# Latent attention with column-tiled score and value matmuls and one eviction for four heads

## Chip, cores and metric

The kernel runs on one core of a Trainium2 chip. The metric is the device time of one execution in microseconds, lower is better. The engines are TensorE (PE, with its weight loads as PEld), VectorE (DVE), ScalarE (ACT), GpSimd (POOL) and SyncE (SP), which issues the DMA transfers.

## The reference

Attention through 32 packed latents per head feeds two feed-forward blocks. All of it is float32.

```python
# q, k, v: 8 x 8 x 576 x 64   p: 8 x 8 x 32 x 64   (batch, heads, sequence, head_dim)
def sm_attn(qq, kk, vv):
    s = scale * np.matmul(qq, kk.transpose(0, 1, 3, 2))
    s = s - np.max(s, axis=-1, keepdims=True)
    a = np.exp(s)
    a = a / (np.sum(a, axis=-1, keepdims=True) + 1e-09)
    return np.matmul(a, vv)
p_packed = sm_attn(p, k, v)                  # the latents: the stage that is changed
out = sm_attn(q, p_packed, p_packed)
...
x = attn_out.transpose(0, 2, 1, 3).reshape(B * S, H * D)       # 4608 x 512
x = _moe_ref(x)     # rms norm, silu(x w_gate) * (x w_val), w_out; hidden 1536
return _moe2_ref(x) # h = x w_in; (h * cos(h)) w_out; hidden 2048
```

## The kernel before, in words

The program has three parts. The first computes the latents p_packed for all batches, four heads at a time: 16 groups (NG), one round of a loop (L535) for each, and two more rounds to finish. The second projects the latents through the gate and value weights, attends with the queries and runs the first feed-forward block. The third runs the second feed-forward block. Everything in the first part runs under a manual schedule, so each engine takes its instructions in the order in which the code issues them.

A round i of the first part works on several groups at once, in this order on TensorE: `u_et(i-1)` transposes the exponentials of the group before (tile et, evicted to eT), `u_s1(i)` multiplies latents with keys (the scores, tile s1, shown as s in the trace), `u_prep(i+1)` transposes the latents of the next group (tile pt), `u_kt(i+1)` transposes its keys in two halves (tile kp, evicted to kT by ScalarE), `u_fin(i-2)` transposes a finished result (tile tp), and `u_pp(i-1)` multiplies exponentials with values (tile pp, evicted to cd by VectorE). Pieces of the query attention of batch 0 (tiles qtp, sp, atp, xp, rp) are put between them.

The latents enter the scores as a block-diagonal operand pbd, so that one matmul over 128 rows serves two heads (64 rows each). There are two such pairs, j = 0 and 1. Before the change, pbd is 384 columns wide and mostly zeros: pair j is multiplied as 128 weight columns, of which 64 hold the two heads, and the second pair is added onto the first in the same PSUM tile. For the values, one matmul takes all four heads' exponentials (128 weight columns) against all four heads' values (256 columns); of the 128 x 256 result only the four diagonal blocks of 32 x 64 are wanted, and four VectorE operations take them out. The exponentials come in six chunks of 96 sequence positions.

Between the maxima and the transposes stands a chain over engines: s to VectorE (maximum, L403 and L404), to ScalarE (exponential e, L411), back to TensorE (et, L423). VectorE and ScalarE also convert weights in this stage (`w_prep`, tiles wy and ny), and GpSimd copies each k tile into another layout (`u_copy`, kc from kn) before TensorE transposes it. Keys and values are loaded a few rounds ahead (`load_k(i+3)`, `load_v(i+2)`, three buffers each), by DMAs that all stand in one SyncE queue, behind weight loads that wait for a buffer.

Of the kernel before, what the change touches and what calls it, by code (L numbers as in the profile page):

```python
# [9 lines left out]
F32 = mybir.dt.float32  # L10
# [3 lines left out]
ALU = mybir.AluOpType  # L14
# [6 lines left out]
def kernel(  # L21
# [14 lines left out]
    nc = tc.nc  # L36
    B, H, S, D = q.shape
    NP = p.shape[2]
# [4 lines left out]
    NC_ = S // CP  # L43
    HALF = S // 2
# [15 lines left out]
    BG_B, KP_B, ET_B, PP_B = 1, 2, 2, 1  # L60
# [114 lines left out]
    u1 = ust.enter_context(tc.tile_pool(name="u1", bufs=1))  # L175
# [5 lines left out]
    ps_1 = pst.enter_context(tc.tile_pool(name="ps_1", bufs=1, space=PSUM))  # L181

    gT = u1.tile([128, H], F32, name="gT")
    ppT = [mid_p.tile([128, 2, H, 128], F32R, name=f"ppT{i}") for i in range(B // 4)]
    pbd = [u1.tile([128, 384], F32, name=f"pbd{i}") for i in range(2)]
    for t in pbd:
        nc.gpsimd.memset(t, 0.0)

# [176 lines left out]
    def u_prep(i):  # L365
        pn, kc = nat_k.pop(i)[0], nat_c.pop(i)
        z = st[i] = {}
        pt = ps_2.tile([128, 128], F32, tag="kp", name="pt")
        nc.tensor.transpose(pt, pn.rearrange("p a d -> p (a d)"), ident)
        for r in range(2):  # L370
            rows = slice(r * 64, (r + 1) * 64)
            src, dst = (
                t[rows].rearrange("p (j x) -> p j x", j=2)[:, :, r * NP:(r + 1) * NP] for t in (pt, pbd[i % 2])
            )
            nc.vector.tensor_copy(dst, src)
        z["kT"], z["kc"] = u4.tile([128, 2, S], F32, tag="kT", name="kT"), kc
# [14 lines left out]
    def u_s1(i):  # L391
        z = st[i]
        kT = z["kT"]
        pb = pbd[i % 2]
        s1 = ps_1.tile([128, 2, 512], F32, tag="s1", name="s1")
        for hf in range(2):
            for j in range(2):
                nc.tensor.matmul(
                    s1[:, hf, :HALF], pb[:, j * 128:(j + 1) * 128], kT[:, j, hf * HALF:(hf + 1) * HALF],
                    start=j == 0, stop=j == 1,  # L400
                )
        mx = u2.tile([128, 4], F32, tag="mx", name="mx")
        nc.vector.tensor_reduce(out=mx[:, 0:1], in_=s1[:, :, :HALF], op=ALU.max, axis=AX.XY)  # L403
        nc.vector.tensor_scalar(out=mx[:, 1:2], in0=mx[:, 0:1], scalar1=-scale, scalar2=None, op0=ALU.mult)  # L404
        z["s1"], z["mx"] = s1, mx
# [23 lines left out]
    def u_pp(i):  # L429
        b, g = divmod(i, 2)  # L430
        z = st[i]
        eT, vn, mx = z["eT"], nat_v.pop(i), z["mx"]
        pp = ps_1.tile([128, 4, D], F32, tag="pp", name="pp", bufs=PP_B)
        for c in range(NC_):
            nc.tensor.matmul(pp, eT[:, c], vn[:, :, c, :], start=c == 0, stop=c == NC_ - 1)  # L435
        cd = u2.tile([128, 2, D], F32, tag="cd", name="cd")
        for h in range(4):
            r = slice(h * NP, (h + 1) * NP)
            src = pp[r, h, :].unsqueeze(1).to_broadcast([NP, 2, D])
            nc.vector.tensor_scalar(out=cd[r], in0=src, scalar1=mx[r, 3:4], scalar2=None, op0=ALU.mult)  # L440
        nc.sync.dma_start(out=c_dram[b][:, g, :], in_=cd[:, 0, :])
        z["cd"] = cd

# [85 lines left out]
    order.enter_context(tc.manual_schedule())  # L529
    u_copy(0)  # L530
    u_prep(0)
    u_kt(0, range(2))
    u_copy(1)
    w_q = [[], []]
    for i in range(NG + 2):  # L535
# [9 lines left out]
        if i < NG:  # L545
            u_s1(i)
        if i + 1 < NG:
            u_prep(i + 1)
            u_kt(i + 1, [0])
# [11 lines left out]
        if 0 < i <= NG:  # L561
            u_pp(i - 1)
# [126 lines left out]
    def gv_block(b, hf, f):  # L689
        w = wm_t[b, f // 2]  # L690
        a = ap_t[b, hf]
        fo = (f % 2) * 128
        pss = []
        for gv in range(2):
            ps = ps_gv.tile([128, HALF], F32, tag="mm", name=f"gv{gv}")
            for kt in range(2):
                mm3(
                    ps, w[gv][:, 0, kt, fo:fo + 128], w[gv][:, 1, kt, fo:fo + 128],
                    a[:, 0, kt], a[:, 1, kt], kt == 0, kt == 1,
                )  # L700
            pss.append(ps)
        t = f2.tile([128, HALF], F32, tag="silu", name="silu")
        nc.scalar.activation(out=t, in_=pss[0], func=AF.Sigmoid)
        nc.vector.tensor_tensor(out=t, in0=t, in1=pss[0], op=ALU.mult)  # L704
        nc.vector.tensor_tensor(out=t, in0=t, in1=pss[1], op=ALU.mult)  # L705
        return t
# [129 lines left out]
    for i in range(len(seq) + LAG):  # L836
        b, hf, f = seq[min(i, len(seq) - 1)]
        j = i % B1
        if i < len(seq):
# [12 lines left out]
            t = gv_block(b, hf, f)  # L852
# [8 lines left out]
        if i >= LAG:  # L861
            acc_block(*seq[i - LAG])
            att_step(2 * i + 1)
            b, hf, f = seq[i - LAG]
# [15 lines left out]
            b, hf, f = seq[min(i, len(seq) - 1)]  # L880
# [97 lines left out]
    for i in range(len(seq) + LAG_B):  # L978
        if i < len(seq):
            n, f = seq[i]  # L980
# [9 lines left out]
        if LAG_B <= i < len(seq) + LAG_B - T_END:  # L990
            n, f = seq[i - LAG_B]
# [33 lines left out]
```

## Time and profile before

| what | value |
|---|---|
| time, median of 3 runs | 1802.52 us |
| lowest and highest run | 1800.96 and 1807.84 us |
| profiled execution, first to last instruction (span) | 1799.0 us |
| span below the median of the runs | 3.5 us |
| TensorE busy over the span | 1709.1 us (95%) |
| VectorE, ScalarE, GpSimd busy | 1142.5, 895.8, 317.7 us |
| last eviction cd of the first part | ends at 167.6 us |

Busy times are sums over instructions of one profiled execution. Matmuls are pipelined, so a busy TensorE may still wait for its own results. An fp32 matmul appears as two records, each with a weight load; records of one matmul overlap the next, so the duration of a record is longer than the place that it takes in a row of matmuls. The granted clock of TensorE is a share of its full 2.4 GHz.

### The profile page before, as it was taken

The numbers are of one execution on the slowest core, as the hardware profiler recorded it, in microseconds if no ns is written. First come the engines' busy times: TensorE is split into PE (matmuls) and PEld (weight loads), VectorE is DVE, ScalarE is ACT, GpSimd is POOL, SyncE is SP. The second block draws the span as 40 slices with busy tenths as digits, with TensorE's granted clock in tenths as the row PEclk, the third lists the DMA queues.
The fourth block names the chain that finished last, engine by engine and source line by source line (L and its number), as shares of the span: only waits on it lengthen the run. The fifth ranks groups of instructions, "written<-read, shape, count | busy, mean of one in ns | idle before, by whom it ended". The sixth has DMA issues, their size and how long they took to land.

```text
span 1799.0 us, 26870 instructions
## 1 busy us (share of the span) xinstructions
PE 1709.1 (95%) x10144; PEld 1532.1 (85%) x10144; DVE 1142.5 (64%) x2188; ACT 895.8 (50%) x1725; POOL 317.7 (18%) x250
## 2 busy tenths in 40 slices
PE   7887787879999999999999999999999999999998
PEld 5665687879999999999999988888888888888887
DVE  3676488747676767676656756565656556555554
ACT  3445665534444444444444645454545555454444
POOL 3333666540303030303031300000000000000000
PEclk9988888989999999999999999999999999999999
DMA  9973677744343434343213401010101010100000
GB/s 221 240 191 112 192 243 219 216 148 140 92 139 90 136 94 138 94 140 91 101 55 118 138 1 48 0 48 0 47 1 48 1 47 14 34 1 24 1 24 24
DMA packets 119980, 166.92 MB, mean 93 GB/s; under 512 B 26921, under 2 KB 84265, under 8 KB 119849
## 3 DMA queue, kind: packets, MB, share of 16 engines
q1 hardware_dynamic: 119848, 165.19, 31.0%
q8 instruction: 80, 1.31, 0.3%
q14 instruction: 52, 0.42, 0.1%
HBM read 108.79 MB, written 53.22 MB: 90 GB/s over the span
## 4 chain that ended last, share of the span: by engine, by line
PE 79%; DVE 7%; DMA 7%; ACT 3%; issue 2%; SPq 1%; POOL 1%; ACTq 0%; DVEq 0%; POOLq 0%
PE ops L156 7%; PE ops L154 7%; PE hp L156 7%; PE hp L154 7%; PE hp L155 7%; PE ops L155 7%; PE acc L154 4%; PE acc L155 4%; PE acc L156 4%; PE gv L154 4%; PE gv L156 4%; PE gv L155 4%; DMA m<-ev 2%; PE pp L435 2%; DMA raw<-in_moe_w_in_dram 2%
## 5 line engine op out<-in xcount | busy, mean ns | idle before, releaser
L154 PE MATMUL gv<-apt,wmhl 128*128 128x288 f32 x768 | 233.6, 304 | 11.2 <-DVE silu L704 8.6
L154 PE MATMUL acc<-shl,wohl 128*128 128x288 f32 x768 | 237.1, 309 | 4.7 <-ACT wohl L106 4.5
L155 PE MATMUL acc<-shl,wohl 128*128 128x288 f32 x768 | 231.5, 301 | 0.1
L156 PE MATMUL acc<-shl,wohl 128*128 128x288 f32 x768 | 230.9, 301 | 0.5 <-POOL wohl L107 0.5
L156 PE MATMUL gv<-apt,wmhl 128*128 128x288 f32 x768 | 226.8, 295 | 1.8 <-POOL wmhl L107 1.8
L155 PE MATMUL gv<-apt,wmhl 128*128 128x288 f32 x768 | 227.1, 296 | 0.0
L154 PE MATMUL ops<-w2hl,ghl 128*128 128x512 f32 x576 | 224.2, 389 | 0.0
L155 PE MATMUL hp<-xhl,wmhl 128*128 128x512 f32 x576 | 224.1, 389 | 0.0
L156 PE MATMUL hp<-xhl,wmhl 128*128 128x512 f32 x576 | 224.1, 389 | 0.0
L155 PE MATMUL ops<-w2hl,ghl 128*128 128x512 f32 x576 | 224.1, 389 | 0.0
L154 PE MATMUL hp<-xhl,wmhl 128*128 128x512 f32 x576 | 224.1, 389 | 0.0
L156 PE MATMUL ops<-w2hl,ghl 128*128 128x512 f32 x576 | 222.7, 389 | 0.0
L107 POOL TENSOR_TENSOR wmhl<-wmraw,wmhl 128x512 fp32r<-128x512 f32 x100 | 128.4, 1305 | 512.9 <-ACT wmhl L106 505.6
L945 DVE TENSOR_TENSOR r<-r,hp 128x512 f32<-128x512 f32 x144 | 98.9, 687 | 186.6 <-ACT r L944 186.6
L943 ACT ACTIVATE r<-r 128x512 f32<-128x512 f32 x144 | 91.0, 632 | 247.6 <-DVE r L942 247.6
L106 ACT ACTIVATE shl<-silu 128x288 fp32r<-128x288 f32 x192 | 85.3, 444 | 241.1 <-DVE silu L705 239.9
L938 ACT ACTIVATE kk<-hp,magic 128x512 f32<-128x512 f32 x144 | 99.3, 689 | 122.5 <-PE hp L156 122.5
L154 PEld LDWEIGHTS gv<-apt,wmhl 128*128 128x128 f32 x768 | 144.9, 189 | 13.8 <-DVE silu L704 10.5
L154 PEld LDWEIGHTS acc<-shl,wohl 128*128 128x128 f32 x768 | 148.2, 193 | 5.0 <-ACT wohl L106 4.6
L155 PEld LDWEIGHTS acc<-shl,wohl 128*128 128x128 f32 x768 | 148.6, 194 | 0.6 <-DVE shl L107 0.5
L156 PEld LDWEIGHTS acc<-shl,wohl 128*128 128x128 f32 x768 | 147.9, 193 | 0.9 <-POOL wohl L107 0.9
L156 PEld LDWEIGHTS gv<-apt,wmhl 128*128 128x128 f32 x768 | 144.6, 188 | 2.8 <-POOL wmhl L107 2.8
(138 smaller groups left out, 3494.7 us busy)
## 6 DMA issues: line engine op xcount, KB each, us to landing
wmraw<-m SPq DMA_DIRECT2D x42, 512.0 KB
m<-ev SPq DMA_DIRECT2D x24, 512.0 KB, 5.4
x_dram<-x SPq DMA_DIRECT2D x40, 288.0 KB, 3.4
kn<-in_k_dram SPq DMA_DIRECT2D x16, 576.0 KB, 6.5
vn<-in_v_dram SPq DMA_DIRECT2D x16, 576.0 KB, 8.2
qnat<-in_q_dram SPq DMA_DIRECT2D x32, 288.0 KB, 6.3
m<-ev SPq DMA_DIRECT2D x24, 384.0 KB
x1raw<-x_dram SPq DMA_DIRECT2D x18, 512.0 KB, 4.1
```

The source lines that it names most:

```text
L106: nc.scalar.activation(out=hi, in_=src, func=AF.Copy)
L107: (eng or nc.vector).tensor_tensor(out=lo, in0=src, in1=hi.bitcast(F32), op=ALU.subtract)
L154: nc.tensor.matmul(ps, lhi, rhi, start=first, stop=False)
L155: nc.tensor.matmul(ps, lhi, rlo, start=False, stop=False)
L156: nc.tensor.matmul(ps, llo, rhi, start=False, stop=last)
L435: nc.tensor.matmul(pp, eT[:, c], vn[:, :, c, :], start=c == 0, stop=c == NC_ - 1)
L938: nc.scalar.activation(out=kk, in_=hp, func=AF.Identity, scale=1.0 / TWO_PI, bias=magic[:, 0:1])
L943: nc.scalar.activation(out=r, in_=r, func=AF.Abs)
L945: nc.vector.tensor_tensor(out=r, in0=r, in1=hp, op=ALU.mult)
```

## The change

The score matmuls use 64 weight columns for each pair of heads and write each pair to its own 64 PSUM rows. Nothing is added up, and pbd shrinks to 2 x 64 columns. The value matmuls are split by head: 24 instead of six, each with 32 weight columns and 64 moving columns, writing each head to its own 32 PSUM rows, all in the same 64 PSUM columns. The four evictions become one over all 128 rows. In the built program the score matmuls then use the array as two column tiles of 64, the value matmuls as four column tiles of 32; the transposes around them still use all 128.

```diff
-    pbd = [u1.tile([128, 384], F32, name=f"pbd{i}") for i in range(2)]
+    pbd = [u1.tile([128, 2, 2 * NP], F32, name=f"pbd{i}") for i in range(2)]
...
-                t[rows].rearrange("p (j x) -> p j x", j=2)[:, :, r * NP:(r + 1) * NP] for t in (pt, pbd[i % 2])
+                t[:, :, r * NP:(r + 1) * NP] for t in (pt[rows].rearrange("p (j x) -> p j x", j=2), pbd[i % 2][rows])
...
                 nc.tensor.matmul(
-                    s1[:, hf, :HALF], pb[:, j * 128:(j + 1) * 128], kT[:, j, hf * HALF:(hf + 1) * HALF],
-                    start=j == 0, stop=j == 1,
+                    s1[j * 64:(j + 1) * 64, hf, :HALF], pb[:, j], kT[:, j, hf * HALF:(hf + 1) * HALF],
+                    start=True, stop=True,
                 )
...
-        pp = ps_1.tile([128, 4, D], F32, tag="pp", name="pp", bufs=PP_B)
+        pp = ps_1.tile([128, D], F32, tag="pp", name="pp", bufs=PP_B)
         for c in range(NC_):
-            nc.tensor.matmul(pp, eT[:, c], vn[:, :, c, :], start=c == 0, stop=c == NC_ - 1)
+            for h in range(4):
+                r = slice(h * NP, (h + 1) * NP)
+                nc.tensor.matmul(pp[r], eT[:, c, r], vn[:, h, c, :], start=c == 0, stop=c == NC_ - 1)
         cd = u2.tile([128, 2, D], F32, tag="cd", name="cd")
-        for h in range(4):
-            r = slice(h * NP, (h + 1) * NP)
-            src = pp[r, h, :].unsqueeze(1).to_broadcast([NP, 2, D])
-            nc.vector.tensor_scalar(out=cd[r], in0=src, scalar1=mx[r, 3:4], scalar2=None, op0=ALU.mult)
+        nc.vector.tensor_scalar(
+            out=cd, in0=pp.unsqueeze(1).to_broadcast([128, 2, D]), scalar1=mx[:, 3:4], scalar2=None, op0=ALU.mult
+        )
```

No instruction changes its place on any engine; their number and shape change. On TensorE, a round early in the first part, from the transposes of one group's keys to the scores of the next (s_ is tile s1 with its number, and the last figures are rows by columns of one matmul's result):

```order
 L385 MATMUL kp<-ident,kc 128x96 x12
-L435 MATMUL pp<-vn,eT 128x256 x6
+L437 MATMUL pp<-vn,eT 32x64 x24
 L423 MATMUL et<-ident,e 96x128 x6
-L398 MATMUL s_368<-kT,pbd_166 128x288 x4
+L398 MATMUL s_383<-kT,pbd_166 64x288 x4
 L369 MATMUL pt<-ident,pn 128x128
```

Six matmuls of 256 columns became 24 of 64 columns, the four of the scores write 64 rows each, and both still stand between the same transposes.

On VectorE, the same round, around the eviction of pp:

```order
 L375 COPY pbd_166<-pt 64x2x32 x2
-L440 TENSOR_SCALAR cd<-pp,mx 32x128 x4
+L439 TENSOR_SCALAR cd<-pp,mx 128x128
 L426 TENSOR_SCALAR mx<-mx 128x1
 L427 RECIPROCAL mx<-mx 128x1
-L403 TENSOR_REDUCE mx<-s_368 128x1
+L403 TENSOR_REDUCE mx<-s_383 128x1
```

Four evictions of 32 rows became one of 128, in the same place ahead of the next maximum.

## Rows read from the trace of the kernel before

**Rows 1.** The page, first line: the span.

```profile
span 1799.0 us, 26870 instructions
```

**Rows 2.** Windows: length, busy by engine, granted clock, DMA share, GB/s.

```profile
0.00:168.75 168.75, 136.90 (x736) 108.25 (x736) 102.58 (x269) 74.73 (x198) 52.40 (x47) 0.94 0.74 189
...
360.00:1799.00 1439.00, 1420.67 (x8394) 1282.07 (x8394) 903.61 (x1694) 708.36 (x1311) 143.41 (x115) 1.00 0.21 65
```

**Rows 3.** Groups by line and shape, 5 to 168 us: busy, mean ns.

```profile
L435 PE MATMUL pp<-vn,eT 96*128 96x256 f32 x192 | 52.0, 428 | 0.0
...
L398 PE MATMUL s<-kT,pbd 128*128 128x288 f32 x128 | 35.7, 424 | 0.0
...
L440 DVE TENSOR_SCALAR cd<-pp,mx 32x128 f32<-32x128 f32 x64 | 22.0, 344 | 24.6 <-PE pp L435 23.9
```

**Rows 4.** The chain that ended last: start us, length us, what.

```profile
10.68 3.89 PE s L398 x8
...
61.70 1.94 PE s L398 x8
...
66.79 2.62 PE pp L435 x12
...
69.65 0.66 PE et L423 x6
70.31 1.94 PE s L398 x8
```

**Rows 5.** Tile pp: durations min/median/max in ns.

```profile
L435 PE MATMUL pp<-vn,eT x192: 377/379/687, 22.3 to 165.7; 96*128 96x256 f32 x192
```

**Rows 6.** Timeline near 110 us: start, length, engine, what.

```profile
109.96 1.33 DVE L440 TENSOR_SCALAR cd<-pp,mx 32x128 f32<-32x128 f32 x4
...
111.01 0.27 PE L369 MATMUL pt<-ident,pn 128*128 128x128 f32 x1
...
112.78 0.76 DVE L403 TENSOR_REDUCE mx<-s 128x1 f32<-128x576 f32 x1
```

**Rows 7.** DMA queue from 10 to 100 us; timeline rows of one k tile.

```profile
q1 hardware_dynamic: 18752, 21.00, 92.3%
...
60.43 0.33 SPq L341 DMA_DIRECT2D kn<-in_k_dram  x1
...
68.94 1.46 POOL L355 COPY kc<-kn 96x1536 f32<-96x1536 f32 x1 [6.89 <-DMA kn<-in_k_dram]
...
72.20 0.41 PE L385 MATMUL kp<-ident,kc 96*128 96x96 f32 x3
```

**Rows 8.** Timeline at the end of the first part.

```profile
159.88 1.43 DVE L440 TENSOR_SCALAR cd<-pp,mx 32x128 f32<-32x128 f32 x4
...
161.63 4.47 PE L435 MATMUL pp<-vn,eT 96*128 96x256 f32 x12
...
166.13 1.43 DVE L440 TENSOR_SCALAR cd<-pp,mx 32x128 f32<-32x128 f32 x4 [3.14 <-PE pp L435]
...
167.62 0.33 PE L448 MATMUL tp<-ident,cd 128*128 128x128 f32 x1 [1.53 <-DVE cd L440]
...
168.89 2.57 ACT L106 ACTIVATE stk<-wy 64x512 fp32r<-64x512 f32 x4
```

**Rows 9.** Windows around falls of the clock, and one pp there.

```profile
93.00:97.00 4.00, 3.20 (x21) 2.20 (x19) 2.86 (x8) 2.73 (x8) 0.02 (x1) 0.98 0.96 257
97.00:100.00 3.00, 3.00 (x9) 2.34 (x8) 1.01 (x2) 2.34 (x5) 1.31 (x1) 0.50 0.78 225
111.00:114.00 3.00, 1.00 (x8) 0.62 (x6) 2.85 (x9) 0.82 (x2) 0.00 (x0) 0.98 0.93 277
...
95.99 4.47 PE L435 MATMUL pp<-vn,eT 96*128 96x256 f32 x12
```

**Rows 10.** Short passes: sp in the chain, rp in the timeline.

```profile
75.15 0.99 PE sp L237 x12
...
152.30 0.59 PE L304 MATMUL rp<-ones,ssq 128*96 128x1 f32 x6
...
201.10 1.09 PE L304 MATMUL rp<-ones,ssq 128*96 128x1 f32 x6 [1.79 <-DVE ssq L298]
```

## The prediction

> **What bounds the kernel now.** I read first where the changed lines lie, by the windows of three stretches. All of them lie in the first 168.75 us of a span of 1799.0 us, in which TensorE is busy 137 us, the granted clock is 0.94 and DMA 0.74 of its time; after 360 us TensorE is busy 99% [rows 1, 2]. Nothing behind 168.75 us is edited, and its first ScalarE work (the stk copy at 168.89) stands behind the last latents on ScalarE's queue [rows 8]. So what the stage gains or loses is handed on whole, and the work behind it is taken as unchanged. The question is what sets the length of a round of this stage.
>
> Second, the groups by line give the sizes: 16 rounds with 12 pp passes (mean 428 ns as recorded), 8 passes for s (424 ns) and four cd evictions (344 ns each) [rows 3]. A recorded matmul is longer than the place it takes, since the next one starts before its end; the places are read from the chain that ended last: 12 pp passes take 2.62 us (218 ns each) and 8 passes of s 1.94 us (242 ns each) [rows 4]. An fp32 matmul leaves two records, so these are 6 and 4 matmuls. From one s to the next, 61.70 to 70.31, are 8.61 us, and s and pp hold 4.56 of them; the other 4.05 are transposes and short waits, which the change leaves alone.
>
> Third, the waits that could take TensorE's place. VectorE is late in a few rounds: at 111.01 TensorE has gone on past s to the next transpose, but VectorE takes the maximum only at 112.78, 1.8 us later, behind its four cd evictions and the softmax rows of the queries [rows 6]. DMA is close behind TensorE: between 10 and 100 us the queue holds 92.3% of the 16 engines. The k tile issued at 60.43 is copied by GpSimd at 68.94 (its wait ended with the landing); the copy ends 1.46 us later, at 70.40, and TensorE wants it at 72.20 [rows 7]. That leaves 1.8 us of slack over two rounds.
>
> **The change, part by part.**
>
> *Scores (s).* Four matmuls stay, each with 64 weight columns on half of the PSUM rows. No row shows two matmuls on different columns of the array at once. Bounds: no overlap, 1.94 us as now; all overlapped, half, 0.97. I take a third value: the two passes of one fp32 matmul use the same columns and follow each other, and the second may run beside the first pass of the next head pair. Then four matmuls take five places of 242 ns: 1.21 us, a gain of 0.73 a round.
>
> *Values (pp).* 6 matmuls over 256 columns become 24 over 64, so 12 passes become 48 (and 12 weight loads 48). By the pp row, 64 columns are a quarter of 218 ns, 54.5 ns a pass. Without overlap 48 passes take 2.62 us, nothing won. Four heads at once: 0.65. By the same reasoning as for s: 25 places, 1.36 us, a gain of 1.26. Above lies a bound from the densest short passes in the trace: 12 passes of sp over 64 columns take 0.99 us, some 82 ns a pass, which would make 3.94 us. That row is set by its weight loads of 96 columns and not by issue, since passes of one column (rp) behave alike and stretch with the clock: 0.59 us for six at full clock, 1.09 at half [rows 10]. The loads here have 32 columns, so I stay with the row that the work resembles most, pp itself.
>
> *Changing the shape of the array.* Each round now goes from full to half columns and back, and to quarter columns and back: four changes. What one costs no row shows; from nothing to a full tail of a matmul: pp is recorded at 379 ns and takes 218, so 0.16 us of each lies under the next [rows 5]. I take the upper end, 0.16 a change and 0.64 a round, because the transposes around it run on the full array and every overlap in the trace is between matmuls of that one shape. The Trainium skill (TensorEngine Tiling (Array Packing), Key Properties) says that changing the tiling mode drains TensorE, which speaks against this change; no run here shows it yet. By that rule the 0.64 stands; without it the forecast would be some 2 us lower, since only the rounds that DMA does not hold would gain.
>
> *One eviction (cd).* Four operations on 32 rows become one on 128 rows with as many elements a row. 344 ns each, 1.33 to 1.43 us for the four; one is taken at 0.35, a gain of 1.08 on VectorE. In most rounds it is hidden under et and s (2.6 us of TensorE work between pp and the next maximum), and costs and gives nothing there. It counts where VectorE is late: two rounds (109 to 132 us), 1.05 each, 2.1 us.
>
> *A round on TensorE alone* gains 0.73 + 1.26 - 0.64 = 1.35 us.
>
> *What DMA takes back.* In the ten rounds from 18 to 101 us (8.29 us each) k must land two rounds ahead: the slack of 1.8 us allows 0.9 a round, and a queue at 92.3% leaves 7.7% of 8.29, 0.64. I take 0.75 a round, 7.5 us in place of 13.5. GpSimd's copy of k would then be late next, and TensorE's first transpose of k behind it. The two rounds from 132 to 150 us, when the loads are nearly done, keep 1.35 each: 2.7.
>
> *The first round and the last.* The first s runs at half clock (8 passes in 3.89 us) and is alone on the chain: about 1.2 [rows 4]. At the end everything is in sequence: s gives 0.73, each of two cd 1.08 (159.88 and 166.13), and pp at 161.63 runs at half clock in 4.3 us, against 2 x 1.36, a gain of 1.55 [rows 8]; less three changes of shape, 3.9 in all.
>
> *The clock.* The granted clock falls to 0.50 (1.2 GHz) behind stretches with little but transposes (111 to 114: TensorE busy a third; 93 to 97: 80%), and pp is what pays: 4.47 us at 95.99 in place of 2.62 [rows 9]. Four of 16 pp take 4.3 to 5.0 us for this now, the first at 95.99 and the last at 161.63 [rows 8, 9]. The change takes matmuls away and leaves transposes, so I double the falls: four more, each 1.36 us (a pp of 1.36 at half speed): 5.4 lost.
>
> Sum: 7.5 + 2.7 + 1.2 + 2.1 + 3.9 - 5.4 = 12.0 us. The profile's span is 1799.0, the median of three runs 1802.5, 3.5 above it; the sum is taken off that: **1790.5 us**. A measurement of this kernel can tell about 0.5%, 9 us, from no change.
>
> **Rivals.**
>
> *No overlap on the array.* The passes of different columns run one behind another: s and pp cost as now, and changes of shape 0 to 0.64 a round. Twelve rounds lose 0 to 7.7, the late VectorE rounds give 2.1, the tail 2.2: 1798 to 1806 us. For it: no row shows overlap. Against it: a third value for s and pp needs no more than that separate columns work apart. The Trainium skill (TensorE: Matmul & The Clock Gate, Measured speedup vs the span model) gives 2.38 times for three column tiles; no run here shows that yet.
>
> *Slower: issue.* TensorE's sequencer cannot hand out 96 short instructions (48 passes with their loads) in 1.4 us. The trace proves only 41 ns an instruction (82 a pass). At that price pp takes 3.94, 1.32 more than now, against 0.73 from s and 0.64 for shape: 1.23 more in each of twelve rounds, 14.8, less 4.3 at the VectorE rounds and the tail, plus about 2 there for longer pp: about 1815 us. With s as I take it, and shape and clock charged, it decides from about 2.5 us a pp, 52 ns a pass: above that the change loses. The Trainium skill (TensorE: Matmul & The Clock Gate, Wait — 56ns, not 53.3ns?) has about 62 ns a matmul where instructions are decoded in microcode; by that pp would take an estimated 2.98 us and the time would stay near that of before; sp's passes at 82 ns do not exclude it.
>
> *DMA does not hold the rounds.* Peaks of the queue go well above its mean, and if k lands in time all twelve rounds keep 1.35, or more if a change of shape is cheap (up to 2 us): 1775 to 1785 us.
>
> *The clock stays low.* If most s and pp of twelve rounds run at half speed, 1.21 + 1.36 more a round, some 31 us against 17: about 1816 us; half of that gives no change.
>
> **How the numbers follow.** Forecast (1785 to 1796): 0.42, two thirds of it below 1793.5. DMA not in the way (1772 to 1785): 0.17. No overlap: 0.20, nearly all within 0.5%. Issue: 0.11, slower. Clock: 0.10, most of it slower. Faster 0.28 + 0.17 = 0.45; within 0.5%: 0.14 + 0.18 + 0.02 = 0.34; slower 0.21. The range leaves out a tenth at each end: from 1773 (the third rival near its best) to 1812 (between no overlap with full price of shape and issue).
>
> **What would show it.** Right: the chain has s at about 1.2 us and pp at about 1.4 a round, one cd of about 0.35, the first stk copy on ScalarE at about 157 us in place of 168.89, and between 20 and 100 us waits of GpSimd's k copy or of TensorE for it. Wrong: pp in 2.6 us or more (no overlap, or issue; issue shows as pass starts 60 to 80 ns apart at full clock), gaps of TensorE at each change of shape beyond 0.16, or a granted clock under 0.9 before 90 us. If the stage ends 12 us earlier and the time does not, the reason lies behind the stage, where I assumed none.

## The result, and the profile after

| kernel | median | lowest to highest | runs |
|---|---|---|---|
| before | 1802.11 us | 1800.76 to 1807.84 | 5 |
| changed | 1789.95 us | 1783.12 to 1792.45 | 5 |

The ratio is 0.992, with a 95% interval of 0.9899 to 0.9942. 1790.5 us was forecast, 1773 to 1812 as the range. The profiled execution of the changed kernel is its fastest run, 1783.12 us with a span of 1781.3, so its trace shows more gain than the median does.

The stage first. Its window in the changed kernel, up to where ScalarE takes its first stk copy (columns as in [rows 2]):

```profile
0.00:154.29 154.29, 110.90 (x1312) 76.83 (x1312) 83.13 (x221) 75.79 (x198) 50.63 (x47) 0.79 0.83 207
```

The stage ends at 154.29 in place of 168.89, 14.6 us earlier [rows 2, 8]. TensorE is busy 26 us less in it, but its granted clock fell from 0.94 to 0.79. What lies behind takes 1627.0 us (1781.3 less 154.29) in place of 1630.1. Over the fourteen profiles of this study (the kernel before, the changed one and twelve experiments) the stage ends between 150.92 and 173.23, and that rest takes 1626.6 to 1630.4 us, whatever the stage did: a gain of the stage is handed on whole, and nearly all the difference between profiles is the stage's. The changed kernel alone has 1627.0 and, in a later repetition, 1630.4, so the 3.1 us here are scatter.

One round of the changed kernel at full clock, by the timeline of TensorE (start, length, what):

```profile
57.16 0.82 PE L423 MATMUL et<-ident,e 128*96 128x128 f32 x6
57.91 1.19 PE L398 MATMUL s<-kT,pbd 128*64 128x288 f32 x8
59.03 0.33 PE L369 MATMUL pt<-ident,pn 128*128 128x128 f32 x1
...
61.94 0.41 PE L227 MATMUL qtp<-ident,qnat 96*128 96x96 f32 x3
62.28 0.88 PE L437 MATMUL pp<-vn,eT 96*32 96x64 f32 x48
63.09 0.47 PE L227 MATMUL qtp<-ident,qnat 96*128 96x96 f32 x3
...
64.14 1.19 PE L398 MATMUL s<-kT,pbd 128*64 128x288 f32 x8
```

From one s to the next, 57.91 to 64.14, are 6.23 us, where [rows 4] have 8.61. s takes 1.12 (57.91 to 59.03) in place of 1.94, pp 0.81 (62.28 to 63.09) in place of 2.62. The eight passes of s fill four places of 242 ns, 0.97 us, and 0.15 more; the 48 passes of pp fill twelve places of 54.5 ns, 0.65, and 0.16 more. So all tiles work side by side. Changes of shape show at both ends: s ends 0.15 and pp 0.16 later than its places fill, and each begins 0.09 to 0.10 later behind the transposes (et to s 0.75 in place of 0.66, qtp to pp 0.34 in place of 0.24).

If all 16 rounds ran like this, the stage would be some 39 us shorter (0.73 net for each s, 1.71 for each pp). It is 14.6. The starts of s in both timelines show where the lead is won and lost:

| s of group | before | changed | lead |
|---|---|---|---|
| 1 | 18.04 | 17.42 | 0.6 |
| 4 | 42.33 | 36.46 | 5.9 |
| 5 | 52.19 | 50.85 | 1.3 |
| 7 | 70.15 | 64.14 | 6.0 |
| 8 | 81.80 | 78.05 | 3.8 |
| 9 | 91.15 | 89.40 | 1.8 |
| 11 | 109.07 | 105.49 | 3.6 |
| 13 | 132.43 | 125.72 | 6.7 |
| 15 | 150.25 | 141.33 | 8.9 |
| first stk copy | 168.89 | 154.29 | 14.6 |

The lead is lost in two places, between groups 4 and 5 and between 7 and 9. (In the profile of the repetition, which took 1787.59 us, the first loss is there too; the second is not.) The waits of TensorE from 10 to 100 us (engine, tile and line, what it waited for: total, times, longest):

```profile
PE sp L237 <- DMA bq<-q: 4.6, 1, 4.6
PE kp L385 <- POOL kc L355: 3.0, 1, 3.0
```

Before, the first was 0.3 us and the second was not there. The chain that ended last shows what stands behind the second (start, length, what):

```profile
58.36 8.59 DMA kn<-in_k_dram
...
67.09 1.47 POOL kc L355
68.60 0.76 PE kp L385 x3
...
78.12 2.12 PE s L398 x8
```

The k tile issued at 58.36 lands 8.6 us later, GpSimd copies it, and TensorE stands still from 65.6 to 68.6. After that s takes 2.12 us and no longer 1.12. Before, the same tile was issued at 60.43, landed as quickly (8.5 us) and was wanted at 72.20 [rows 7]. So TensorE now wants it 6.6 us earlier, but it leaves only 2.1 us earlier. Ahead of it in SyncE's queue stands a weight load, which waited for VectorE's conversion of older weights (waits from 50 to 59 us):

```profile
SPq L115 <- DVE wy L149: 3.2, 1, 3.2
```

Before, that wait was 3.0 us. The windows on both sides of the stall (columns as in [rows 2]):

```profile
55.00:65.00 10.00, 9.11 (x161) 6.71 (x159) 7.09 (x20) 6.87 (x20) 2.91 (x2) 1.00 1.09 275
70.00:90.00 20.00, 18.14 (x171) 13.79 (x173) 12.04 (x27) 8.83 (x23) 7.35 (x5) 0.50 1.09 255
```

From 70 to 90 us TensorE is busy 91% of the time and yet has the lower clock, 1.2 GHz, throughout. A round there takes 11.4 us (s of group 8 to s of group 9, 78.05 to 89.40), where the same round took 9.4 before (81.80 to 91.15). The DMA share is 1.09 on both sides.

### The profile page after: what moved, and what is told of

It reads as the page before. It is cut to its first block, busy times and chain, and to the rows that moved or that the text cites. A ratio compares the mean times of both kernels' runs of the same rounds, so it can differ in the third digit from the quotient of the medians.

```text
span 1781.3 us, 27979 instructions
## 1 busy us (share of the span) xinstructions
PE 1681.4 (94%) x10720; PEld 1500.2 (84%) x10720; DVE 1123.5 (63%) x2140; ACT 897.7 (50%) x1725; POOL 315.5 (18%) x250
## 4 chain that ended last, share of the span: by engine, by line
PE 77%; DMA 9%; DVE 6%; ACT 3%; SPq 2%; issue 2%; POOL 1%; ACTq 0%; DVEq 0%; POOLq 0%
PE ops L156 7%; PE ops L154 7%; PE hp L155 7%; PE hp L154 7%; PE ops L155 7%; PE hp L156 7%; PE acc L154 4%; PE acc L155 4%; PE acc L156 4%; PE gv L154 4%; PE gv L155 4%; PE gv L156 4%; DMA wmraw<-m 2%; DMA m<-ev 2%; DMA raw<-in_moe_w_in_dram 1%
```

## The experiments

The theory to be tested: column tiles work side by side, which shortens TensorE's rounds by about 2.4 us, and DMA and the clock take most of it back. Rival one: the gain is the single eviction's, on VectorE. Rival two: short passes are quick by themselves, not because they overlap.

**Scores alone** (with the smaller pbd; values and evictions as before).

```diff
-                    s1[:, hf, :HALF], pb[:, j * 128:(j + 1) * 128], kT[:, j, hf * HALF:(hf + 1) * HALF],
-                    start=j == 0, stop=j == 1,
+                    s1[j * 64:(j + 1) * 64, hf, :HALF], pb[:, j], kT[:, j, hf * HALF:(hf + 1) * HALF],
+                    start=True, stop=True,
```

> The scores by 64-column tiles alone; values and the four evictions as before. Theory (the column tiles work side by side, and DMA and the clock take most of it back): s about 1.12 us a round at full clock instead of 1.94, pp 2.62 as before; time 1795 to 1799 us. Rival one (the gain is that of the single eviction on VectorE): s short, but the time within 2 us of before, 1800 to 1804.

Measured: 1801.58 us, ratio 1.0004 (0.999 to 1.0017). There is no gain, although s is as short as in the changed kernel (37.45 to 38.57 in its timeline). The theory missed by 2.6 us (1795 to 1799), and rival one had the time. Its timeline shows where much of the 0.73 us a round went:

```profile
51.09 2.15 PE L237 MATMUL sp<-bq,qT 128*96 128x64 f32 x12 [1.39 <-DMA bq<-q]
53.03 4.68 PE L435 MATMUL pp<-vn,eT 96*128 96x256 f32 x12
```

There is a wait for bq of 1.4 us, and a long pp behind it at half clock; the granted clock from 10 to 100 us is 0.92 where the kernel before had 0.98. Eight of the 16 pp take 4.3 to 5.4 us, where four did before (for one of the eight, at 23.93, the profile gives a clock of 1.00 all the same). Against 2.78 us, the eight lose 16.8 us in all and the four 7.5. That is 9.3 of the 11.7 us that 16 rounds of 0.73 would have given, in this one profile.

**Values and eviction** (scores and pbd as before).

```diff
-                    s1[j * 64:(j + 1) * 64, hf, :HALF], pb[:, j], kT[:, j, hf * HALF:(hf + 1) * HALF],
-                    start=True, stop=True,
+                    s1[:, hf, :HALF], pb[:, j * 128:(j + 1) * 128], kT[:, j, hf * HALF:(hf + 1) * HALF],
+                    start=j == 0, stop=j == 1,
```

> The values by 32-column tiles and the single eviction; scores as before. Theory: pp about 0.81 us at full clock, s 1.94; some 1.7 us a round on TensorE, of which DMA leaves a part: 1789 to 1794 us, close to the changed kernel, since DMA holds the first ten rounds either way. Rival one: 1794 to 1797, the eviction's share alone.

Measured: 1786.26 us, ratio 0.9911 (0.9892 to 0.993), the same as the changed kernel within the intervals. That is 3 us below the theory's 1789 to 1794, and further below rival one's 1794 to 1797. Its pp has the recorded median of 219 ns a pass, as in the changed kernel. So no gain of the scores' part can be seen, alone or with the rest, and the values and the eviction carry the gain. The clock differs: its six runs have a mean granted clock of 0.973 to 0.979 over the span, the eleven runs of the changed kernel (five, and six in the repetition) 0.965 to 0.973.

**Four evictions** (the changed kernel otherwise).

```diff
-        nc.vector.tensor_scalar(
-            out=cd, in0=pp.unsqueeze(1).to_broadcast([128, 2, D]), scalar1=mx[:, 3:4], scalar2=None, op0=ALU.mult
-        )
+        for h in range(4):
+            r = slice(h * NP, (h + 1) * NP)
+            src = pp[r].unsqueeze(1).to_broadcast([NP, 2, D])
+            nc.vector.tensor_scalar(out=cd[r], in0=src, scalar1=mx[r, 3:4], scalar2=None, op0=ALU.mult)
```

> The changed kernel with four evictions of 32 rows in place of one. Theory: loses 1.08 us in the two or three rounds that VectorE holds and twice at the end, 3 to 5 us in all: 1793 to 1795. Rival one: loses nearly the whole gain, 1798 to 1802.

Measured: 1792.80 us, ratio 0.9958 (0.9944 to 0.9972). That is 3 to 5 us above the changed kernel's medians (1789.95, and 1788.28 in a later repetition, ratio 0.9925, 0.9901 to 0.9949), the size that the theory had; its interval just overlaps the repetition's, so that the eviction adds anything is likely and not shown by the times. Rival one is out, since most of the gain stays without the single eviction.

**All heads' values in one column tile.** The passes keep their size and number, but use the same 32 columns.

```diff
-        pp = ps_1.tile([128, D], F32, tag="pp", name="pp", bufs=PP_B)
-        for c in range(NC_):
-            for h in range(4):
-                r = slice(h * NP, (h + 1) * NP)
-                nc.tensor.matmul(pp[r], eT[:, c, r], vn[:, h, c, :], start=c == 0, stop=c == NC_ - 1)
+        pp = ps_1.tile([128, 4, D], F32, tag="pp", name="pp", bufs=PP_B)
+        for h in range(4):
+            r = slice(h * NP, (h + 1) * NP)
+            for c in range(NC_):
+                nc.tensor.matmul(pp[:NP, h], eT[:, c, r], vn[:, h, c, :], start=c == 0, stop=c == NC_ - 1)
...
+            src = pp[:NP, h].unsqueeze(1).to_broadcast([NP, 2, D])
+            nc.vector.tensor_scalar(out=cd[r], in0=src, scalar1=mx[:NP, 3:4], scalar2=None, op0=ALU.mult)
```

> The changed kernel, but all four heads' values are written to PSUM rows 0 to 31 (in 4 x 64 columns), so all 48 passes use the same 32 columns of the array; four evictions, scaled by the first head's factors (the other heads' normalisation is left out). The passes have the same size and number as in the changed kernel. Theory (overlap of different columns): pp 2.6 us a round or more, 54 ns a pass or more; stage some 15 us longer, 1797 to 1803. Rival two (short passes are quick by themselves, wherever they stand): pp 0.8 to 1.0 us, time like the kernel with four evictions, about 1794.

Measured: 1810.79 us, ratio 1.0053 (1.0033 to 1.0073), 18 us above the kernel with four evictions, which differs only in the tile, the order of heads and chunks, and the rows that the evictions read. Its timeline, at full clock and at a fall of it:

```profile
74.29 2.87 PE L437 MATMUL pp<-vn,eT 96*32 96x64 f32 x48
77.09 0.47 PE L227 MATMUL qtp<-ident,qnat 96*128 96x96 f32 x3
...
104.24 4.49 PE L437 MATMUL pp<-vn,eT 96*32 96x64 f32 x48
```

The same 48 passes take 2.80 us (74.29 to 77.09) in one tile and 0.81 in four, 3.5 times as long. Rival two falls; the overlap is shown. In time it cost more than the theory had given (1797 to 1803). Seven of its pp ran at half clock, where each takes over 4 us; that this is the reason is argued and not shown.

**DMA's part: an extra copy of 288 KB in rounds 1 to 9**, in the changed kernel and in the kernel before.

```diff
+        if 1 <= i < 10:
+            nc.sync.dma_start(out=extra[i - 1], in_=q[0, 0:2].rearrange("h (p c) d -> p h c d", c=NC_))
         load_k(i + 3)
```

> The changed kernel with a copy of 288 KB more in each of rounds 1 to 9, from one place in memory to another, which nothing waits for. Theory (DMA holds the first ten rounds): 2.6 MB at some 240 GB/s are 11 us, and all of it shows: 1798 to 1802. Rival (the clock alone holds them): 2 to 4 us, 1791 to 1794.

> The kernel before with the same extra copies. Theory: the slack of its queue (7.7% of 90 us, and 1.8 us of lead over two rounds) takes up half or more of the 11 us: 1804 to 1808, so the lead of the changed kernel shrinks by 4 us or more. Rival: the same 2 to 4 us as with the changed kernel.

Measured: 1790.59 us, ratio 0.9934 (0.9911 to 0.9957), with the changed kernel, and 1803.29 us, ratio 1.0006 (0.9989 to 1.0023), with the kernel before. The first lies 0.6 to 2.3 us above the changed kernel's medians, where the theory had 11; the second 1 us above. The theory misses for both, and both times lie 0.4 to 1 us below what the rival gave as well. The queue of the changed kernel with the copies, from 10 to 100 us (packets, MB, share of 16 engines):

```profile
q1 hardware_dynamic: 20013, 22.61, 99.0%
```

In the changed kernel that row has 21.34 MB at 96.7%, in its repetition 22.02 MB at 98.7%, and the queue of before stood at 92.3% [rows 7]. A queue whose share is nearly 1 took another 0.6 to 1.3 MB in the same 90 us. So its share does not say how many bytes more it can carry, and the bandwidth alone does not hold these rounds. The copies are not free all the same: in this profile TensorE's waits for k and bq are 12.9 us (10 to 160 us), where the changed kernel's two profiles have 7.6 and 8.1.

**DMA's part: the round trip.** The query attention of batch 0 begins a round later, so that its latents have longer to go to memory and back.

```diff
-    ATT_U, U_ATT, U_ATT_N = 26, 3, 2
+    ATT_U, U_ATT, U_ATT_N = 26, 4, 2
```

> The changed kernel with the query attention of batch 0 begun one round later (U_ATT 4 in place of 3), so that the latents have a round more to come back from memory. Theory (waits for DMA round trips take back the matmuls' gain): TensorE's wait of 4.6 us for bq, at 40 to 45 us, is gone; the stage ends 2 to 4 us earlier and the time is 1785 to 1788. Rival (the queue's bandwidth alone holds the first 100 us): the wait moves to k, the time stays at 1788 to 1791.

Measured: 1785.93 us, ratio 0.9906 (0.9885 to 0.9928). The median is where the theory had it, but the interval overlaps the changed kernel's, and the rest did not go as it said. The stage ends at 154.73, where the changed kernel's two profiles have 154.29 and 155.44. The waits of TensorE from 10 to 160 us:

```profile
PE kp L385 <- POOL kc L355: 5.4, 4, 2.1
...
PE sp L237 <- DMA bq<-q: 2.5, 1, 2.5
```

Of the 4.6 us for bq 2.5 are left, and the waits for k grew from 3.0 (3.4 in the repetition) to 5.4. The wait moved on, as the rival said; the time does not decide.

**The clock's part: two full-array matmuls ahead of each pp.**

```diff
-        pp = ps_1.tile([128, D], F32, tag="pp", name="pp", bufs=PP_B)
+        pq = ps_1.tile([128, 4, D], F32, tag="pp", name="pp", bufs=PP_B)
+        for c in range(2):
+            nc.tensor.matmul(pq, eT[:, c], vn[:, :, c, :], start=True, stop=True)
+        pp = pq[:, 0]
```

> The changed kernel with two of the old value matmuls (full array, 256 columns, four passes of 218 ns) ahead of each pp, into the same bank; their result is overwritten. They add 0.87 us a round at full clock. Rival (the clock is what takes the gain back): the granted clock from 10 to 100 us rises from 0.78 to 0.90 or more and the time falls or stays within 3 us in spite of 14 us more work. Theory (DMA first, the clock second): the clock rises, the first ten rounds hide the work, the time is 1788 to 1795.

Measured: 1784.93 us, ratio 0.9906 (0.9885 to 0.9926). The window from 10 to 100 us:

```profile
10.00:100.00 90.00, 78.44 (x841) 53.74 (x840) 43.13 (x122) 45.33 (x122) 29.34 (x20) 0.92 0.99 240
```

The granted clock is 0.92, in place of 0.77 and 0.82 in the changed kernel's two profiles, and 14 us more of TensorE work (16 x 0.87) made the time no longer. That is what the rival, the clock, had expected; the time is below the theory's 1788 to 1795. But TensorE's waits for bq and k are 3.0 us here, in place of 7.6 and 8.1: part of the added work stands where TensorE had waited. So this run does not tell the clock from the waits.

**Together, and in a gap.** Three variants ran beside the changed kernel on one chip: the full-array matmuls and the later attention together; two full-array matmuls of 128 columns in a gap where TensorE waits for ScalarE in any case; and the latter with the later attention.

```diff
+                if list(js) == [0] and hf == 0 and i > 1:
+                    pq_next.append(ps_1.tile([128, 4, D], F32, tag="pp", name="pp", bufs=PP_B))
+                    for _ in range(2):
+                        nc.tensor.matmul(pq_next[0][:, 0:2], ident, ident, start=True, stop=True)
```

> The kernel with two old value matmuls ahead of each pp, and the query attention of batch 0 begun a round later. If the clock and the round trip are separate losses, both gains add: 1779 to 1783 us. If the wait only moves on to k, 1784 to 1787.

> The changed kernel with two full-array matmuls of 128 columns (identity by identity, 0.44 us at full clock, result overwritten) in each round between the two halves of the first transposed keys, where TensorE waits 0.56 us for ScalarE in any case. Clock theory: the granted clock from 10 to 100 us rises above the 0.77 of the changed kernel and the time falls by 3 to 8 us, since the work itself costs nothing there. Rival (DMA holds these rounds): the clock may rise, the time stays within 2 us of the changed kernel.

> The two full-array matmuls in the gap, and the query attention of batch 0 begun a round later. If both losses add: 1777 to 1783 us, the fastest of all; if the wait moves on to k: 1784 to 1787.

> The changed kernel itself, to stand beside the other three on one chip: 1786 to 1791 us, stage end at 154 to 158 us, granted clock from 10 to 100 us below 0.85.

| kernel | median | ratio to before | interval |
|---|---|---|---|
| changed, again | 1788.28 us | 0.9925 | 0.9901 to 0.9949 |
| full-array matmuls, later attention | 1788.54 us | 0.9927 | 0.9901 to 0.9952 |
| matmuls in the gap | 1782.48 us | 0.9893 | 0.9870 to 0.9916 |
| matmuls in the gap, later attention | 1782.72 us | 0.9897 | 0.9877 to 0.9918 |

The repetition came out as expected: 1788.28 us, the stage's end at 155.44, and this window from 10 to 100 us:

```profile
10.00:100.00 90.00, 69.78 (x822) 47.80 (x825) 46.63 (x125) 46.48 (x126) 29.76 (x20) 0.82 0.99 246
```

The two with matmuls in the gap have the lowest medians of the study, 5.6 to 5.8 us under the changed kernel and 1.0 to 1.1% under the kernel before. In time both met a stated expectation: the gap alone the clock theory's 3 to 8 us lower, with the later attention 1777 to 1783. Their intervals overlap the changed kernel's, so that they beat it is likely and not shown. The full-array matmuls with the later attention missed their 1779 to 1783 and their 1784 to 1787. Their seven runs lie far apart, from 1780.07 us at a mean clock of 0.980 to 1796.12 us at 0.973. The profile is of the first of these, the fastest execution that was profiled: the window from 10 to 100 us

```profile
10.00:100.00 90.00, 77.35 (x920) 52.68 (x918) 48.59 (x134) 48.61 (x132) 32.63 (x22) 1.00 1.02 255
```

has a granted clock of 1.00 and 255 GB/s, and its stage ends at 150.92. The profile of the gap kernel is the opposite, its slowest run of six (1790.72 us):

```profile
10.00:100.00 90.00, 70.96 (x833) 51.05 (x831) 43.67 (x122) 44.11 (x119) 27.37 (x19) 0.83 1.00 227
```

It has 227 GB/s at nearly the same share, and its TensorE waits 13.0 us for GpSimd's copy of k in four stalls from 10 to 160 us. Its clock of 0.83 is no higher than the repetition's 0.82, so this profile does not show the rise that the clock theory expected; over the whole span, though, its six runs have 0.971 to 0.974, the repetition's six 0.965 to 0.973, and the gap with the later attention has 0.91 from 10 to 100 us in its profile. The rates differ by 12% at a full share, between two kernels that do not load the same tiles in that window (238 and 246 in the changed kernel's own two profiles). Of these two kernels the one at the lower rate has the longer waits; that the rate makes the waits, and the waits the clock, is not shown (with the extra copies the rate was 253 GB/s and the waits were 12.9 us).

## Why the prediction was right, and which of its terms were not

The median came out 0.6 us from the forecast, and that closeness is luck. The mechanism held in its outline: column tiles overlap, the stage's gain is handed on, and DMA waits and the clock take most of it back. The reason given for the DMA term did not hold, and several terms were off, in both directions. One of the prediction's own signs of being wrong came true, a granted clock under 0.9 before 90 us: it is 0.78 from 10 to 90.

*Handed on whole.* Right: the rest is 1626.6 to 1630.4 us in all fourteen profiles. Of the 17.7 us between the two spans, 14.6 are the stage's and the rest is within that scatter.

*Scores and values.* Overlap was right and was taken too small. The prediction let only one pass of each matmul run beside the next head's: 1.21 us for s and 1.36 for pp. In fact all tiles run at once: s takes 1.12 and pp 0.81, the tail at the end included. The densest row before, 82 ns a pass, was rightly not put down to issue: passes here start 17 ns apart on average (0.81 us over 48). That its weight loads set it is not shown.

*Changes of shape.* 0.64 us a round were charged, 0.50 measured (0.09 to 0.10 going in, 0.15 to 0.16 coming out, twice). The Trainium skill (TensorEngine Tiling (Array Packing), Key Properties) says that changing the tiling mode drains TensorE. The trace agrees in kind, with these costs at either end. The cost is paid out of a gain about six times its size (2.9 us a round). With these, a round of TensorE alone gains 2.4 us and not 1.35.

*The eviction.* It was to give 2.1 us in the late VectorE rounds and 2.2 at the end, together 4.3; without it the time is 3 to 5 us longer. From group 11 to 13, the rounds that VectorE held, the lead grows by 3.1. One eviction has 346 ns, as taken.

*DMA and the clock.* This is the term that was mis-sized most. DMA was to leave 7.5 us in ten rounds and the clock to take 5.4 over the stage. In the trace the lead grows from 0.6 at group 1 only to 3.6 at group 11, 3.0 us in these ten rounds, where TensorE at full clock would have won 24. The place was right: the copy of k is what is late next, and TensorE behind it. But the reason given, a queue with 7.7% to spare, was wrong: a further 2.6 MB cost 1 to 2 us and not 11. What costs are single late landings, 3.0 us of wait for k and 4.3 more for bq than before, and the half clock that follows them, for 20 us at a stretch behind the second. The prediction had the falls as four more pp of 1.36 us, eight in all. Seven pp ran at half clock, but each takes 1.44 in place of 0.81 and so loses only 0.6; what it left out is the other work of these rounds, since everything from 70 to 90 us ran at half clock, transposes and sp too. In this profile, against rounds that win 2.4 us each, groups 4 to 5 lose 7.0 us and groups 7 to 9 lose 9.0. The two stalls are 7.3 of these 16; the other 8.7 are, by estimate, the half clock's.

*The first and the last rounds.* The lead at group 1 is 0.6, where 1.2 was forecast, and from group 13 to 15 it grows by 2.2 of 2.7. From group 15 to the first stk copy it grows by 5.7, where 3.9 was forecast, for the most part since pp at half clock shrinks from 4.3 to 1.5 and not to 2.7.

So larger gains (1.35 taken, 2.4 found) met larger losses, and the sum stood near by the two errors' cancelling. Of the rivals, no overlap and issue are out by measurement. DMA not in the way is out as well: the fastest run (1783.12) lies in its range, but its trace has the waits for k and bq. The clock staying low came true in part: in the profile of the scores alone, which give 1.0004, long pp hold 9.3 of the 11.7 us to be gained.

*What stays open* is how the loss divides between clock and waits over many executions. Within the changed kernel's five runs the mean clock says nothing about the time (0.967 for 1783.12 us, 0.970 for 1789.95, 0.966 for 1792.45). In the repetition's six it does (0.973 for 1782.19 us, 0.965 for 1793.18), and in eleven of the twelve experiments slower runs have on the whole the lower clock (correlations of -0.6 to -0.9). The two go together; which comes first, these numbers do not show. Full-array matmuls go with a higher clock and leave the time about where it is, or 6 us lower, in intervals that overlap. A kernel with k loaded earlier, which would take away the waits by themselves, was not tried.

## What to carry to other kernels

Small fp32 matmuls on different columns of the array run side by side: give each group of output rows its own column tile, and price a pass by the tile that has most to do, plus a quarter of a microsecond for each excursion from the full array. Before counting on the gain, look at what was second: here a k tile had 1.8 us of slack over two rounds, and the shorter rounds ran into it. A load that stands behind others in a queue leaves when they let it, however early the engine that wants it gets there (2.1 us earlier here, where 6.6 were wanted). A single stall then costs more than itself, when the clock falls behind it. To remove the first stall before shortening the work around it further follows from this, but was not tried here. Look at a part's gain alone, as the scores' part gave none.

## What the runs showed of the hardware

- 48 fp32 passes of 64 columns with 48 weight loads of 32 columns take 0.81 us over four column tiles at full clock, 1.44 at half clock (84.64 to 86.08 in the changed kernel's chain) and 2.80 in one tile at full clock. 96 instructions in 0.81 us are 8.4 ns each, so their issue took no more than that.
- TensorE kept the lower clock for 20 us while it was busy 91% of the time, with transposes, column-tiled matmuls and sp, after a stall of 3.0 us. Two matmuls on the whole array in each round went with a clock of 0.92 in place of 0.77 and 0.82 from 10 to 100 us.
- DMA at a share of 0.97 to 1.02 of 16 engines moved 227, 238 and 255 GB/s from 10 to 100 us in the profiles of three kernels (matmuls in the gap; changed; full-array matmuls with later attention). A full share is not a full rate.
